# Four products of state and input weights computed in the first pair and kept in HBM, with new due steps for the first pair

## The chip, the cores and the metric

The kernel runs on one core of a Trainium2 chip. Its time is the device time of the whole program in microseconds (us), from several runs. Beside these there is one profiled execution, from which all lines of the profile come. Engines are called PE (TensorE, matrix products), PEld (its weight loads), DVE (VectorE), ACT (ScalarE), POOL (GpSimd) and SP (SyncE, whose queue issues nearly all DMAs).

## The reference

A cross attention between tokens and a small state, in both directions, whose outputs are laid together and go through a gated layer. `x` and `state` are float32; `w_in` (512 x 2048) and `w_out` (2048 x 512) are float64.

```python
B, H, S, Ns, D = 8, 8, 512, 32, 64           # x: (B,H,S,D), state: (B,H,Ns,D)
a  = softmax(scale * x @ state.T);  xread = a @ state      # 512 rows per batch
a2 = softmax(scale * state @ x.T);  sread = a2 @ x         # 32 rows per batch
y = concat([xread, sread], axis=2) -> (B*(S+Ns), H*D)      # 4352 x 512
h = y @ w_in;  g = h * cos(h);  out = g @ w_out            # 4352 x 2048, 4352 x 512
```

## The kernel before, in words

**The token rows.** `xread` is never formed. For each batch the state of each head is multiplied with the rows of `w_in` of that head ("products": 8 small matmuls of 64 rows and 32 columns, which run beside each other on PE, for 512 columns of `w_in`), so that `h` is the product of the attention weights `aT` with these products `sw`. A batch needs four such products, `nt` = 0 to 3, one for each 512 columns. `Attention.products(nt)` makes one in two banks of PSUM, either `at` or `side_banks`; `products_kept(nt)` copies it with ACT to `sw_all[:, nt % 2]`. So `sw_all` has two slots, used in turn, and product `nt` + 2 can be written there when the tiles of product `nt` have read it. "(b, nt)" below is product `nt` of batch `b`.

**Tiles.** A tile is 128 columns of `h` for the 512 tokens of a batch: 16 tiles to a batch, four to a product. A tile goes through `hidden` (PE), `gate` (ACT, rounding), `gate2` (DVE), `gate3` (ACT, sine) and `gate4` (DVE), which writes `g_all`. From batch 2 on, two tiles are taken together and done with seven half-size products in place of eight (`seven_part`); four sums of `sw`, made by POOL three steps ahead (`sw_sums`), serve them. `g` times `w_out` is done for two batches at once ("pair"), as seven products p1 to p7 of half size, each again of seven stages; their 49 weight blocks lie in HBM in `blocks_kept` and are fetched by SP into a ring of four.

**Two planners.** A step is one tile; 128 steps for the tokens, then 16 for the state rows.
- *The first pair* (batches 0 and 1, steps 0 to 31). It also loads and converts the float64 weights: each piece is loaded raw and converted by two operations of ACT, two of DVE and one of POOL. The w_out blocks' sums and their stores to `blocks_kept` are made here too, and the first five stages of p5 with the first tile pair of batch 2. The first two products with `w_out` are done plainly here, eight steps each: `first` (into `held` slot 0) and `second` (into slot 1, `second_kept`; its result is stored). All work is listed as tasks with a cost, what they read and write, and a due step. `first_pair` turns due steps to times (22 + PACE x step), passes them back along dependencies, and takes on each engine, among tasks that can start within NEAR, the one due first. Tasks that use the same buffer keep the order in which they are listed. `FIRST` = 32 and `now[0]` is 31 here.
- *The later pairs* (from step 32). The program is written step by step to a tape; `in_order` orders it again by a model of costs. `plan(b)` says at which step of a batch its products are made: (b, 1) at 0, (b, 2) at 3, (b, 3) at 8, (b + 1, 0) at 12. There the banks `at` are used.

`held` has three slots of 128 x 2 x 512 for partial results of the output (slot 0 is first the raw state).

Of the kernel before, what the change touches and what calls it, by code (L numbers as in the profile page):

```python
# [10 lines left out]
F32 = mybir.dt.float32  # L11
# [11 lines left out]
def kernel(  # L23
# [44 lines left out]
    nc = Lanes  # L68
# [42 lines left out]
    def matrix(n):  # L111
# [7 lines left out]
            for i in range(NB)]  # L119
    spare = ctx.enter_context(tc.tile_pool(name="spare", bufs=1,  # L120
                                           space=bass.MemoryType.DRAM))
    blocks_kept = spare.tile([7, 8, P, QT * P], F32)

    xT = consts.tile([P, NK, S], F32)
    ots_all = [consts.tile([P, S], F32, name=f"ot{i}") for i in range(2)]
    n_stored = [0]
    x_b = consts.tile([P, NC, H, D], F32)
# [157 lines left out]
    class Attention:  # L285
# [891 lines left out]
    def first_pair_tasks():  # L1177
# [49 lines left out]
        def attention(b, k):  # L1227
# [89 lines left out]
        def products(b, nt, k, c0=0, c1=WC):  # L1317
# [16 lines left out]
            for j in range(2):  # L1334
# [5 lines left out]
                        nc.vector.tensor_copy if taken else None, (j,)),  # L1340
                    side[j], sw[j], k)

        def tile_(t, k):
            n = t.b * NF + t.f
            h, z, c = n % 2, t.b % 2, t.f // 4 % 2
            g = names(quads_of[t.row][t.i // QT], t.i % QT)
            add("pe", 1.72, lambda: hidden(t),
                f"sw{c}{t.f % 4 // 2}0 sw{c}{t.f % 4 // 2}1 z{z}0 z{z}1",
                f"h{h} H", k)
            add("act", act(512) - .04, lambda: gate(t), f"h{h}", f"q{h}")  # L1350
            add("dve", dve(512) - .02, lambda: gate2(t), f"h{h} q{h}", f"q{h}")
            add("act", .63 if n else 1.91, lambda: gate3(t), f"q{h} T",
                f"q{h}")
            add("dve", dve(512) - .02, lambda: gate4(t), f"h{h} q{h}", g,
                k + 2)

        def inner(which, m, q, temps, to, k, raw=True):
            for i in range(4):
                t = to.split()
                r = (names(q), names(q) + " " + t[0], names(q),  # L1360
                     names(q) + " " + t[1])[i]
                add("pool", pool(512), lambda i=i: inner_weight(m, temps, i),
                    r, t[i], k)
            if raw:
                sends(which, m, q, k + 1)
            for i in range(4):
                add("sp", .4, lambda i=i: send_inner(which, temps, i),
                    to.split()[i], f"B{which}", k + 1)
# [135 lines left out]
                lambda i=i, due=due: conversion(i, due))  # L1504
        for step, what in (
                (1, lambda: attention_late(0, 0)),
                (3, lambda: products(0, 1, 2.5)),
                (3, lambda: add("pe", .4, lambda: states(1, side_banks[0]),
                                "held0", "sd00 sd01", 8.5)),
                (3, lambda: add("act", .53,  # L1510
                                lambda: states_kept(1, side_banks[0]),
                                "sd00 sd01", "stT1", 5.5)),
                (5, lambda: attention(1, 4)),
                (7, lambda: products(0, 2, 4.5)),
                (11, lambda: products(0, 3, 11.5)),
                (13, lambda: products(1, 0, 16)),
                (13, lambda: attention_late(1, 18)),
                (13, lambda: inner(0, a11, 5, temps[0], names(TEMPS), 14.5)),
                (15, lambda: sends(2, a22, 8, 17)),
                (15, lambda: sums_of(SQ, A21, A22, add_, 16, "pool")),  # L1520
                (16, lambda: products(1, 1, 18.5)),
                (16, lambda: inner(3, matrix(SQ), SQ, temps[1], E, 17)),
                (17, lambda: sums_of(A22, SQ, A11, sub_, 16, "pool")),
                (17, lambda: attention(2, 19)),
                (18, lambda: sums_of(A21, A11, A21, sub_, 20, "dve")),
                (20, lambda: products(1, 2, 23)),
                (20, lambda: inner(5, matrix(A21), A21, temps[0],
                                   names(TEMPS), 20)),
                (20, lambda: sends(1, a12, 6, 22)),
                (21, lambda: inner(4, matrix(A22), A22, temps[1], E, 22)),  # L1530
                (23, lambda: sums_of(SQ, A12, A22, sub_, 23, "dve")),
                (24, lambda: inner(6, matrix(SQ), SQ, temps[0], names(TEMPS),
                                   25)),
                (24, lambda: products(1, 3, 31)),
                (25, lambda: attention_late(2, 25)),
                (24, lambda: [add("sp", .4, lambda n=n: fetch_block(n), "B3",
                                  f"ring{n}", 27) for n in range(NB - 1)])):
            at_step[step].append(what)
        t32, t34 = all_tiles[PERIOD], all_tiles[PERIOD + 2]
        for step, what in (  # L1540
                (26, lambda: outer(0, 2, 0, 0, 26, "dve")),
                (27, lambda: outer(0, 2, 0, 1, 27, "dve")),
                (28, lambda: tokens_of_next(32)),
                (28, lambda: products(2, 0, 28)),
                (28, lambda: p5_tasks(30.5)),
                (29, lambda: weight_columns(t32, 30.5)),
                (29, lambda: add("dve", .7, lambda: halves(2, 0), "z00 z01",
                                 "E0", 30, True)),
                (29, lambda: add("dve", .7, lambda: halves(2, 1),
                                 "z00 z01 E0", "E1", 30, True)),  # L1550
                (30, lambda: seven_tasks(t32, 29.5)),
                (31, lambda: weight_columns(t34, 32)),
                (32, lambda: outer(2, 3, 2, 0, 32, "dve")),
                (32, lambda: p3_sums(32))):
# [55 lines left out]
    def first_pair():  # L1610
# [23 lines left out]
        while can:  # L1634
# [28 lines left out]
            if t.shares or t.engine == "pool":  # L1663
                lock = end
            if t.engine == "sp":
                size = {"x": .13, "Q": 1.05, "B": .26, "r": .26}.get(
                    t.writes[0][0], .3)
                lanes = max(lanes, at_ + 1.3) + size / .36
                end = lanes - 1.8
# [296 lines left out]
```

## Time and profile before

| what | value |
|---|---|
| runs | median 719.63 us of 3 (718.04 to 723.23) |
| profiled execution | 716.66 us, its span 714.9 us, granted clock 1.00 |
| products in the later pairs (PE at<-w_in,st_all) | 384 records of 64x512, 16 to a product |
| products in the first pair (PE h<-w_in,st_all) | 112 records of 64x512, 32 of 64x256 |
| ACT copies of products from at / from h | 48 / 16 |
| HBM read, written | 87.03 MB, 23.59 MB |
| first pair on PE | to about 151 us |

The busy time of an engine is the union of its instructions; a matmul record has 379 ns for 256 columns[...]. Each matmul in float32 appears as two records. Where a line ends in brackets, they hold the idle time of that engine just before it and the engine and tile whose end released it.

### The profile page before, as it was taken

The page shows a single profiled execution, that of the slowest core. Times are in us where ns is not written, and L with a number is a line of the kernel's source. Part 1 is how long each engine was busy: PE and PEld are TensorE (multiplying, and loading weights), DVE is VectorE, ACT ScalarE, POOL GpSimd, SP SyncE. Part 2 cuts the span into 40 slices and gives each one's busy share as a digit, 9 for nine tenths or more (in the row PEclk, how much of TensorE's full clock was granted, in tenths as well). Part 3 has the DMA queues.
Part 4 walks back from the last instruction along what each step waited for, and adds up shares of the span by engine and source line. Part 5 has one row for each costly group of instructions (what it writes and reads, how often), then busy time and mean ns, then how long its engine had stood idle before and what let it go on. Part 6 is the DMA issues. An engine that isn't in the chain of part 4 may idle for free.

```text
span 714.9 us, 10741 instructions
## 1 busy us (share of the span) xinstructions
PE 696.3 (97%) x3628; PEld 520.8 (73%) x3628; DVE 487.8 (68%) x698; ACT 348.2 (49%) x591; POOL 518.7 (73%) x524
## 2 busy tenths in 40 slices
PE   8898799999999999999999999999999999999997
PEld 3344344477878787787778788877888888888886
DVE  4999879977867578877776576868765465624430
ACT  5789876754544465443744473345444443211100
POOL 1565799576889988798889746789888748695500
PEclk9999999999999999999999999999999999999999
DMA  9966699765458744772369337843365344376841
GB/s 296 298 209 197 193 265 292 177 154 142 125 138 180 192 139 114 148 174 79 93 133 196 92 88 140 173 117 89 118 169 141 90 118 118 104 220 169 222 97 30
DMA packets 204022, 111.34 MB, mean 156 GB/s; under 512 B 149888, under 2 KB 166784, under 8 KB 203968
## 3 DMA queue, kind: packets, MB, share of 16 engines
q1 hardware_dynamic: 202880, 110.14, 59.2%
q8 instruction: 29, 0.48, 0.3%
q10 hardware_dynamic: 960, 0.39, 0.2%
q14 instruction: 25, 0.20, 0.1%
q0 software_dynamic: 128, 0.13, 0.1%
HBM read 87.03 MB, written 23.59 MB: 155 GB/s over the span
## 4 chain that ended last, share of the span: by engine, by line
PE 66%; DVE 2%; ACT 1%; POOL 1%; issue 1%; ACTq 0%; DVEq 0%
PE o L51 38%; PE h L51 21%; PE at L51 8%; POOL g_all L51 1%; ACT q_all L51 1%; DVE g_all L51 1%; DVE h L51 0%; DVE q_all L51 0%; DVE xT L51 0%; ACT L51 0%; DVE aT_all L51 0%; DVE held L51 0%; DVE m_all L51 0%; ACT sw_all L51 0%; ACT aT_all L51 0%
## 5 line engine op out<-in xcount | busy, mean ns | idle before, releaser
L51 POOL TENSOR_TENSOR g_all<-g_all 128x512 f32<-128x512 f32 x280 | 354.9, 1296 | 43.2 <-DVE g_all L51 17.5
L51 PE MATMUL o<-g_all 128*128 128x256 f32 (+1 forms) x1560 | 383.9, 391 | 0.0
L51 PEld LDWEIGHTS o<-g_all 128*128 128x128 f32 x1560 | 293.2, 190 | 63.9 <-issue 21.8
L51 ACT ACTIVATE q_all<-h 128x1024 int32<-128x1024 f32 (+1 forms) x88 | 73.2, 831 | 120.8 <-PE h L51 119.2
L51 DVE TENSOR_TENSOR q_all<-q_all,h 128x1024 f32<-128x1024 int32 (+1 forms) x88 | 85.5, 973 | 62.7 <-ACT q_all L51 62.4
L51 PE MATMUL h<-aT_all,sw_all 128*128 128x256 f32 (+1 forms) x320 | 118.1, 469 | 5.4 <-DVE g_all L51 5.4
L51 DVE TENSOR_TENSOR g_all<-h,q_all 128x1024 f32<-128x1024 f32 (+1 forms) x88 | 85.8, 977 | 38.3 <-ACT q_all L51 36.6
L51 ACT ACTIVATE q_all<-q_all,halfpi 128x1024 f32<-128x1024 f32 (+1 forms) x88 | 84.1, 957 | 35.9 <-DVE q_all L51 35.2
L51 PEld LDWEIGHTS h<-aT_all,sw_all 128*128 128x128 f32 x320 | 59.2, 190 | 40.7 <-issue 20.6
L51 DVE TENSOR_TENSOR g_all<-g_all 128x1024 f32<-128x1024 f32 (+1 forms) x78 | 74.3, 993 | 0.1
L51 DVE TENSOR_TENSOR h<-h,sums_all 128x256 f32<-128x256 f32 x96 | 41.1, 428 | 38.5 <-PE h L51 33.5
L51 PE MATMUL h<-aS_all,swS_all 128*128 128x256 f32 x192 | 59.7, 393 | 0.0
L51 PE MATMUL h<-aS_all,sw_all 128*128 128x256 f32 x192 | 57.5, 381 | 1.2 <-DVE h L51 1.0
L51 POOL TENSOR_TENSOR swS_all<-sw_all 128x128 f32<-128x128 f32 x48 | 21.9, 457 | 48.1 <-ACT sw_all L51 28.6
L51 PEld LDWEIGHTS h<-aS_all,swS_all 128*128 128x128 f32 x192 | 34.4, 189 | 21.3 <-issue 8.2
L51 PEld LDWEIGHTS h<-aS_all,sw_all 128*128 128x128 f32 x192 | 35.9, 190 | 7.9 <-DVE h L51 1.6
L51 POOL TENSOR_TENSOR w_in<-w_in,aS_all 128x1024 int32<-128x1024 int32 (+1 forms) x10 | 21.4, 2153 | 27.9 <-ACT m_all L51 14.2
L51 DVE SCALAR_TENSOR_TENSOR held<-o,held 128x512 f32<-128x512 f32 x38 | 26.1, 687 | 15.0 <-PE o L51 14.3
L51 ACT COPY sw_all<-at 128x512 f32<-128x512 f32 x48 | 25.8, 591 | 18.6 <-PE at L51 18.2
L51 ACT COPY o<-o 128x256 f32<-128x256 f32 x26 | 9.3, 359 | 46.7 <-PE o L51 46.6
L51 ACT COPY o<-sums_all 128x256 f32<-128x256 f32 x26 | 9.8, 376 | 44.9 <-PE o L51 44.9
L51 POOL TENSOR_TENSOR g_all<-g_all,aS_all 128x1024 int32<-128x1024 int32 x8 | 20.9, 2627 | 13.6 <-DVE g_all L51 7.2
(99 smaller groups left out, 748.6 us busy)
## 6 DMA issues: line engine op xcount, KB each, us to landing
g_all<-blocks_kept SPq DMA_DIRECT2D x206, 256.0 KB, 2.8
blocks_kept<-g_all SPq DMA_DIRECT2D x48, 256.0 KB, 4.1
g_all<-in_moe_w_out_dram SPq DMA_DIRECT2D x8, 1024.0 KB, 5.7
out_dram<-ot SPq DMA_DIRECT2D x128, 64.0 KB, 2.8
g_all<-in_moe_w_in_dram SPq DMA_DIRECT2D x6, 1024.0 KB, 7.6
x_b<-in_x_dram SPq DMA_DIRECT2D x24, 256.0 KB, 4.8
xT<-in_x_dram SPq DMA_DIRECT2D x80, 64.0 KB, 2.9
x_b<-in_x_dram SPq DMA_DIRECT2D x16, 128.0 KB, 4.0
```

Source lines behind the costliest of these rows:

```text
L51: made = self.last = f(*args, **kw)
```

## The change

- The products (3, 0), (3, 1), (2, 2) and (2, 3) are made in the first pair, in `side_banks`. ACT copies each to a slot of `held` (1 or 2, in turn), and SP sends it from there to a new array `products_early` in HBM (512 KB each).
- In the later pairs these four are not made: `products` returns, and `products_kept` is a DMA by SP from `products_early` into the slot of `sw_all`.
- The due steps of the first pair's tasks are other numbers, as are PACE, NEAR and the spacing passed back along dependencies, the order and due steps of the weight conversions, and the times at which the planner takes the raw weights to have arrived.

```diff
     blocks_kept = spare.tile([7, 8, P, QT * P], F32)
+    EARLY = ((3, 0), (3, 1), (2, 2), (2, 3))
+    EARLY_DUE = (13.61, 17.22, 27.33, 28.44)
+    products_early = spare.tile([len(EARLY), P, 2 * S], F32)
...
         def products(self, nt, bank=None, c0=0, c1=WC):
+            if now[0] >= FIRST and (self.b, nt) in EARLY:
+                return
...
         def products_kept(...):
+            if now[0] >= FIRST and (self.b, nt) in EARLY:
+                nc.sync.dma_start(
+                    out=sw_all[:, nt % 2].rearrange("p j s -> p (j s)"),
+                    in_=products_early[EARLY.index((self.b, nt))])
+                return
...
-    ARRIVED = (10.0, 11.3, 12.7, 14.0, 16.6, 19.3, 22.0)
+    ARRIVED = (10.7, 12.1, 13.5, 14.8, 18.2, 20.9, 23.9)
...
-            m2 = k + 6 if b == 0 else k + 4
+            m2 = k + 6 if b == 0 else k + 8.0
...
+        def products_ahead(n):
+            b, nt = EARLY[n]
+            slot, k = 1 + n % 2, EARLY_DUE[n]
+            w = ("w0 w1 w2 w3", "w4 w5", "w7 w8", "w10 w11")[nt]
+            side = ["sd00 sd01", "sd10 sd11"]
+            add("pe", 1.05, lambda: attn[b].products(nt, 0),
+                w + f" stT{b // 4}", " ".join(side), k)
+            for j in range(2):
+                add("act", act(WC), lambda j=j: nc.scalar.copy(
+                    held[:, slot, j], side_banks[j]), side[j],
+                    f"held{slot}{j}", k)
+            add("sp", .5, lambda: nc.sync.dma_start(
+                out=products_early[n],
+                in_=held[:, slot].rearrange("p j s -> p (j s)")),
+                f"held{slot}0 held{slot}1", f"p{n}", k + 2)
...
             add("dve", dve(512) - .02, lambda: gate4(t), f"h{h} q{h}", g,
-                k + 2)
+                k + 23.5)
...
-                (3, lambda: products(0, 1, 2.5)),
+                (3, lambda: products(0, 1, 8.5)),
...
-                (7, lambda: products(0, 2, 4.5)),
-                (11, lambda: products(0, 3, 11.5)),
-                (13, lambda: products(1, 0, 16)),
-                (13, lambda: attention_late(1, 18)),
+                (7, lambda: products(0, 2, 14.0)),
+                (11, lambda: products(0, 3, 14.0)),
+                (13, lambda: products(1, 0, 21.5)),
+                (13, lambda: attention_late(1, 35.0)),
...
-                (16, lambda: products(1, 1, 18.5)),
+                (16, lambda: products(1, 1, 32.0)),
...
-                (17, lambda: attention(2, 19)),
+                (17, lambda: attention(2, 17.5)),
...
-                (20, lambda: products(1, 2, 23)),
+                (20, lambda: products(1, 2, 24.5)),
...
-                (24, lambda: products(1, 3, 31)),
+                (24, lambda: products(1, 3, 28.5)),
...
-                (28, lambda: products(2, 0, 28)),
+                (28, lambda: products(2, 0, 34.0)),
...
+        for n, due in enumerate(EARLY_DUE):
+            at_step[max(0, int(due) - 1)].append(
+                lambda n=n: products_ahead(n))
...
-                first(step - 4, step - 1)
+                first(step - 4, step + 1)
             for i in range(NH):
                 if SECOND_AT[i] == step:
-                    second(i, step)
+                    second(i, step - 2)
...
-    CONV = (4, 5, 6, 7, 8, 9, 10, 11, 14, 15, 16, 17, 12, 13)
-    CONV_DUE = (3, 4.5, 3.5, 6, 6.7, 8.5, 9, 9.5, 12.0, 11, 11.3, 13.7, 12.5, 15.7)
-    PACE, NEAR, SEND = 3.4, 0.3, 2.5
+    CONV = (4, 6, 5, 7, 9, 8, 10, 11, 14, 15, 16, 17, 13, 12)
+    CONV_DUE = (1.8, 1.5, 1.0, 3.0, 5.3, 5.0, 12.4, 7.7, 14.1, 10.0, 12.0, 16.0, 17.1, 16.4)
+    PACE, NEAR, SEND = 3.2, 0.15, 2.5
...
-                t.due = min(t.due, u.due - t.cost - 0.05)
+                t.due = min(t.due, u.due - t.cost - 0.3)
```

The other due steps that change are those of the sums, stores and inner weights of `w_out`, of the second half of the states, of batch 1's and 2's attention, and of the tasks from step 26 on; the kinds of work are the same.

More of the change, by code (lines that the diff above doesn't have):

```diff
@@ L122 @@
     blocks_kept = spare.tile([7, 8, P, QT * P], F32)
+    EARLY = ((3, 0), (3, 1), (2, 2), (2, 3))
+    EARLY_DUE = (13.61, 17.22, 27.33, 28.44)
+    products_early = spare.tile([len(EARLY), P, 2 * S], F32)
     xT = consts.tile([P, NK, S], F32)
+    hbm_names.append(products_early.name)
     ots_all = [consts.tile([P, S], F32, name=f"ot{i}") for i in range(2)]
@@ L1506, in first_pair_tasks @@
                 (1, lambda: attention_late(0, 0)),
-                (3, lambda: products(0, 1, 2.5)),
+                (3, lambda: products(0, 1, 8.5)),
                 (3, lambda: add("pe", .4, lambda: states(1, side_banks[0]),
-                                "held0", "sd00 sd01", 8.5)),
+                                "held0", "sd00 sd01", 7.0)),
                 (3, lambda: add("act", .53,
                                 lambda: states_kept(1, side_banks[0]),
-                                "sd00 sd01", "stT1", 5.5)),
@@ L1513, in first_pair_tasks @@
-                (5, lambda: attention(1, 4)),
-                (7, lambda: products(0, 2, 4.5)),
-                (11, lambda: products(0, 3, 11.5)),
-                (13, lambda: products(1, 0, 16)),
-                (13, lambda: attention_late(1, 18)),
-                (13, lambda: inner(0, a11, 5, temps[0], names(TEMPS), 14.5)),
-                (15, lambda: sends(2, a22, 8, 17)),
-                (15, lambda: sums_of(SQ, A21, A22, add_, 16, "pool")),
-                (16, lambda: products(1, 1, 18.5)),
@@ L1522, in first_pair_tasks @@
-                (16, lambda: inner(3, matrix(SQ), SQ, temps[1], E, 17)),
-                (17, lambda: sums_of(A22, SQ, A11, sub_, 16, "pool")),
-                (17, lambda: attention(2, 19)),
-                (18, lambda: sums_of(A21, A11, A21, sub_, 20, "dve")),
-                (20, lambda: products(1, 2, 23)),
+                                "sd00 sd01", "stT1", 2.5)),
+                (5, lambda: attention(1, 4.5)),
+                (7, lambda: products(0, 2, 14.0)),
+                (11, lambda: products(0, 3, 14.0)),
@@ new lines, in first_pair_tasks @@
+                (13, lambda: products(1, 0, 21.5)),
+                (13, lambda: attention_late(1, 35.0)),
+                (13, lambda: inner(0, a11, 5, temps[0], names(TEMPS), 17.5)),
+                (15, lambda: sends(2, a22, 8, 17)),
+                (15, lambda: sums_of(SQ, A21, A22, add_, 31.5, "pool")),
+                (16, lambda: products(1, 1, 32.0)),
+                (16, lambda: inner(3, matrix(SQ), SQ, temps[1], E, 16.0)),
+                (17, lambda: sums_of(A22, SQ, A11, sub_, 18, "pool")),
@@ L1527, in first_pair_tasks @@
+                (17, lambda: attention(2, 17.5)),
+                (18, lambda: sums_of(A21, A11, A21, sub_, 22.5, "dve")),
+                (20, lambda: products(1, 2, 24.5)),
                 (20, lambda: inner(5, matrix(A21), A21, temps[0],
-                                   names(TEMPS), 20)),
+                                   names(TEMPS), 23.0)),
                 (20, lambda: sends(1, a12, 6, 22)),
-                (21, lambda: inner(4, matrix(A22), A22, temps[1], E, 22)),
-                (23, lambda: sums_of(SQ, A12, A22, sub_, 23, "dve")),
+                (21, lambda: inner(4, matrix(A22), A22, temps[1], E, 41.0)),
@@ L1532, in first_pair_tasks @@
+                (23, lambda: sums_of(SQ, A12, A22, sub_, 30.0, "dve")),
                 (24, lambda: inner(6, matrix(SQ), SQ, temps[0], names(TEMPS),
                                    25)),
-                (24, lambda: products(1, 3, 31)),
-                (25, lambda: attention_late(2, 25)),
+                (24, lambda: products(1, 3, 28.5)),
+                (25, lambda: attention_late(2, 25.0)),
                 (24, lambda: [add("sp", .4, lambda n=n: fetch_block(n), "B3",
@@ L1540, in first_pair_tasks @@
         for step, what in (
-                (26, lambda: outer(0, 2, 0, 0, 26, "dve")),
-                (27, lambda: outer(0, 2, 0, 1, 27, "dve")),
-                (28, lambda: tokens_of_next(32)),
-                (28, lambda: products(2, 0, 28)),
+                (26, lambda: outer(0, 2, 0, 0, 28.0, "dve")),
+                (27, lambda: outer(0, 2, 0, 1, 32.5, "dve")),
+                (28, lambda: tokens_of_next(32.0)),
+                (28, lambda: products(2, 0, 34.0)),
                 (28, lambda: p5_tasks(30.5)),
-                (29, lambda: weight_columns(t32, 30.5)),
+                (29, lambda: weight_columns(t32, 33.5)),
                 (29, lambda: add("dve", .7, lambda: halves(2, 0), "z00 z01",
@@ L1550, in first_pair_tasks @@
                                  "z00 z01 E0", "E1", 30, True)),
-                (30, lambda: seven_tasks(t32, 29.5)),
+                (30, lambda: seven_tasks(t32, 30)),
                 (31, lambda: weight_columns(t34, 32)),
@@ L1665, in first_pair @@
             if t.engine == "sp":
-                size = {"x": .13, "Q": 1.05, "B": .26, "r": .26}.get(
+                size = {"x": .13, "Q": 1.05, "B": .26, "r": .26, "p": .52}.get(
                     t.writes[0][0], .3)
```

## Prediction

> **What bounds the kernel now.** I read four views: the page, busy time in stretches of 10 us, the tensor engine's (PE's) timeline, and ACT's timeline where PE waits. First the page: busy rows, and slices of 17.9 us.
>
> ```profile
> PE 696.3 (97%) x3628; PEld 520.8 (73%) x3628; DVE 487.8 (68%) x698; ACT 348.2 (49%) x591; POOL 518.7 (73%) x524
> ...
> PE   8898799999999999999999999999999999999997
> ...
> PEclk9999999999999999999999999999999999999999
> ```
>
> PE is the bound, at full clock; slices under 9 lie only at the very end and before 130 us, in the first pair. Stretches there, with the columns PE, weight load, DVE, ACT, POOL, clock, DMA share, GB/s:
>
> ```profile
> 60.00:70.00 10.00, 8.09 (x25) 3.90 (x24) 8.99 (x14) 9.15 (x14) 5.00 (x2) 1.00 0.59 184
> 70.00:80.00 10.00, 7.99 (x46) 2.60 (x45) 9.36 (x14) 8.80 (x16) 6.31 (x3) 1.00 0.61 195
> 80.00:90.00 10.00, 7.77 (x60) 3.50 (x59) 7.79 (x11) 8.98 (x14) 7.90 (x5) 1.00 0.54 159
> ...
> 100.00:110.00 10.00, 10.00 (x47) 4.53 (x45) 8.05 (x10) 4.83 (x9) 9.99 (x6) 1.00 0.69 208
> 110.00:120.00 10.00, 10.00 (x37) 4.00 (x37) 10.00 (x15) 6.31 (x11) 9.84 (x8) 1.00 0.96 283
> ```
>
> From 60 to 92 us ACT and DVE are nearly full and PE has holes; from 92 us on PE is full. The holes in PE's timeline (start, length, operation; in brackets the idle time before it and who ended it):
>
> ```profile
> 67.47 1.98 PE L51 MATMUL h<-aT_all,sw_all 128*128 128x512 f32 x4 [1.91 <-DVE g_all L51]
> ...
> 74.90 1.98 PE L51 MATMUL h<-aT_all,sw_all 128*128 128x512 f32 x4 [1.00 <-DVE g_all L51]
> ...
> 78.91 3.70 PE L51 MATMUL h<-aT_all,sw_all 128*128 128x512 f32 x8 [1.01 <-DVE g_all L51]
> ...
> 87.73 1.09 PE L51 MATMUL at<-x_b,xT 128*64 128x128 f32 x16 [1.16 <-ACT xT L51]
> 89.89 1.98 PE L51 MATMUL h<-aT_all,sw_all 128*128 128x512 f32 x4 [1.07 <-DVE g_all L51]
> ```
>
> PE waits for the last gate operation of an earlier tile (DVE g_all), which frees a bank of h, and once for a copy by ACT. The five holes are 6.15 us. Earlier ones are 2.63, 0.85 and 0.21 us, later ones 0.34 and 0.41: 10.6 us between 20 and 146 us. Filler matmuls (o<-g_all at 20.03, 30.55 and 34.08 us) are 4.0 us more. **The rule of my sum**: PE's work stays as large as it was; four pieces of it move. So the end moves by idle time filled or made, and by nothing else.
>
> **What is removed.** One product of the later pairs, batch 2's third, in PE's timeline:
>
> ```profile
> 171.22 0.59 PE L51 MATMUL h<-aT_all,swS_all 128*128 128x256 f32 x2
> 171.74 1.09 PE L51 MATMUL at<-w_in,st_all 64*32 64x512 f32 x16
> 172.76 1.99 PE L51 MATMUL o<-g_all 128*128 128x256 f32 x8
> 174.59 0.59 PE L51 MATMUL h<-aS_all,sw_all 128*128 128x256 f32 x2
> ```
>
> From start to start it takes 1.02 us. The group before it takes 0.52 where such a pair otherwise takes 0.43, and the eight after it 1.83 where they otherwise take 1.73: 0.19 us more. [...] By the bare row the four products are 4 x 1.02 = 4.1 us, with the switches 4 x 1.21 = 4.84. I take 4.84. [...]
>
> The four stand at 171.74, 197.21, 217.57 and 235.30 us, in a PE that is full, so the 4.84 us leave the path whole. The second has a hole behind it:
>
> ```profile
> 198.44 1.08 ACT L51 COPY sw_all<-at 128x512 f32<-128x512 f32 x2 [2.00 <-PE at L51]
> 199.54 1.28 ACT L51 ACT_TABLE_LOAD   x1
> 200.83 1.15 ACT L51 ACTIVATE q_all<-q_all,halfpi 128x1024 f32<-128x1024 f32 x1
> ```
>
> ACT waited 2.00 us for this product, copied it, and only then loaded the table for the sine; through DVE that ended PE's wait of 0.88 us before 203.70. Without the copies ACT is up to 3 us earlier there and the hole goes: **-0.88**. What is late next is PE itself.
>
> **What is added late: four loads of 512 KB.** Each writes a slot of sw_all as soon as its last reader is done. I read these times from PE's timeline as 165.5, 184.4, 204.2 and 224.3 us, with the next readers 18 to 20 us later. POOL's four sums (0.46 us each) stand between load and reader. The rows for 256 KB:
>
> ```profile
> g_all<-blocks_kept SPq DMA_DIRECT2D x206, 256.0 KB, 2.8
> blocks_kept<-g_all SPq DMA_DIRECT2D x48, 256.0 KB, 4.1
> ```
>
> Twice the bytes land in 2.8 to 5.6 us, my estimate: at least 10 us are spare. Issuing takes SP 0.4 us each. A load that waits for its slot holds the ring fetches behind it on SP; these are issued three stages ahead, about 8 us at 2.7 us a stage (565 us for 206), and land in 2.8, so 5 us of waiting cost nothing. Bounds 0 to 2 us for all four, taken as 0.
>
> **What is added in the first pair.** Per product: 1.21 us of PE, two ACT copies (1.05 us by the pair sw_all<-h at 78.91), one send on SP of 0.4 us. They share the side banks with the others, in the order of listing: batch 3's first product goes between batch 0's fourth (72.8 us) and batch 1's first (76.8), its second between batch 1's second (83.6) and third (115.6), batch 2's pair after batch 1's fourth (126.3).
> - Batch 3's two fall where the holes are: PE 0 (2.42 of the 6.15 us are filled). ACT gets 2.1 us more in a stretch where it is busy 24.87 of 28 us (64 to 92). If all of it delays gates, it costs 2.1; if it fits into ACT's 3.1 us of idle time, 0. I take **+0.6**, nearer to 0: batch 1's first product, copied at 78.91 and first read at 93.43, now has due step 21.5 for 16, and its 1.05 us of copies can leave the stretch.
> - Batch 2's two fall where PE is idle 0.76 us in 54 (92 to 146): **+2.42**. Bounds 0, if later work is pulled into the holes, to 2.42.
> - The sends wait for ACT's copies; behind them on SP stand block sends and token loads, which have 5 us and more. Taken as 0; where it isn't, see the last rival.
>
> **Due steps set anew.** The operations stay, their order changes. Its worth is bounded by idle time: 6.15 - 2.42 + 0.75 = 4.5 us gained if every remaining hole after 60 us closes, 3.8 lost if two new ones like the longest (1.91) open. For a gain speak products copied long before use: batch 0's third ran at 50.52 and was first read at 61.09, with ACT at 9.2 of 10; its due goes from step 4.5 to 14. I take half of the gain: **-2.2**.
>
> **Sum**: -4.84 - 0.88 + 2.42 + 0.6 - 2.2 = -4.9 us. The profiled execution took 716.66 us (span 714.9 and 1.8 around it) and would take 711.8. The runs shown have a median of 719.63, 3 us above the profiled one; the same step from there gives **714.7 us**, 0.7% less.
>
> **Rivals.**
> - *The new order closes the holes.* All of 6.15 + 0.75 goes, half of the 4.0 us of filler, and the 0.88: -9.8, 709.8 us. For it: PE's idle time in 60 to 92 us is larger than what the two products need, and copies done 10 to 15 us early are there to be shifted. Against: ACT is at 89% there, DVE at 81%.
> - *The first pair gives it back.* ACT's 2.1 us delay the gates in full and the new order brings nothing: -4.84 - 0.88 + 2.42 + 2.1 = -1.2, 718.4 us.
> - *Slower: a send holds up the accumulator.* Batch 2's third product is kept in slot 1 of held, listed ahead of the end of the second product, which writes that slot next. ACT's copy of the accumulator (at 125.56 now) then waits until the send has landed; behind it on ACT stand all gates, and p5's first stage on PE (133.65) waits for the bank. If that product runs at 127.5, copies end at 129, and the send lands 4.1 (the row of half its size) to 8.2 us later, the copy ends at 134.6 to 138.7, so p5 starts up to 5.2 us late. [...] the DMA share was 0.97 from 120 to 130 us. With the 9.0 us between p5's first two stages (133.65 and 142.68) no longer covered by tiles 28 to 30, I add 4 us: 9.2 - 2.7 (the sum without the new order) = +6.5, 726 us. It decides when the accumulator's copy starts after about 135. Against it: the planner knows the dependency and can do the product earlier.
> - *That it doesn't do what it says* I exclude: the skip holds from step 32 on, the products in the first pair are made at 31, and all four are planned at steps 35 to 48.
>
> **How the numbers follow.** Forecast 0.49, with its own range 711 to 718; about a quarter of it (0.13) lies under 712.4, the point of 1%, which is about what a measurement of this kernel can tell from no change. Holes closed 0.31, all faster; given back 0.08, all same; slower 0.12, two thirds of it beyond 1%. So faster 0.31 + 0.13 = 0.44, slower 0.08, same the remaining 0.48. The range takes in most of the holes-closed case and the bounds above (ACT's 2.1, the loads' 2): 706.5 to 720.5.
>
> **What would show it.** PE at<-w_in,st_all falls from 384 to 320 and h<-w_in,st_all of 512 columns rises from 112 to 176; ACT sw_all<-at from 48 to 40. The hole before 203.70 is gone, and from the end of the first pair on the kernel takes 5.7 us less. Holes between 60 and 92 us sum to 2 us or less; the step to the later pairs (p5's first stage) comes no later than 134. I am wrong if that stage comes after 137, if new waits for POOL swS_all or sw_all appear on PE after 165, or if the stretch after the first pair is no shorter.

## The result, and the profile after

The changed kernel takes 716.58 us (median of 19 executions, 714.95 to 718.81), the kernel before 719.63 us (19 executions, 716.9 to 723.97). The ratio is 0.9953 with a 95% interval of 0.9936 to 0.997. The forecast was 714.7 us: right in direction, in its range and in the outcome "within 1%", and 1.9 us too low. The profiled execution takes 715.76 us, only 0.9 us less than the one of before (716.66), where the prediction had 711.8. So there are two questions: why an execution at full clock gains so much less than forecast, and where the other 2 us of the medians come from.

The products have moved as planned: 64 records fewer in the later pairs (384 before), 64 more in the first pair (112 before).

```profile
L51 PE MATMUL at<-w_in,st_all 64*32 64x512 f32 x320 | 22.1, 600 | 0.0
L51 PE MATMUL h<-w_in,st_all 64*32 64x512 f32 x176 | 12.0, 600 | 0.6 <-ACT sw_all L51 0.6
```

A record has 600 ns, and PE's timeline has the 16 records of a product within 1.09 us (161.73 us): so the eight matmuls of a product do run beside each other.

The page of the changed kernel, the rows of PE:

```profile
PE 698.5 (98%) x3632; PEld 522.6 (73%) x3632; DVE 487.5 (68%) x698; ACT 348.8 (49%) x591; POOL 515.5 (72%) x524
...
PE   8799899999999999999999999999999999999997
```

A slice is 17.9 us. The fourth and fifth, from 54 to 89 us, rose from 8 and 7 to 9 and 8; the second, from 18 to 36 us, fell from 8 to 7. In stretches of 10 us (PE, weight load, DVE, ACT, POOL, clock, DMA share, GB/s):

```profile
30.00:40.00 10.00, 7.14 (x48) 2.96 (x47) 6.75 (x13) 8.70 (x11) 4.65 (x3) 1.00 1.18 318
...
60.00:70.00 10.00, 10.00 (x25) 4.44 (x24) 8.13 (x11) 9.09 (x13) 5.08 (x2) 1.00 0.60 210
70.00:80.00 10.00, 9.30 (x69) 3.31 (x67) 9.11 (x15) 9.25 (x16) 5.07 (x3) 1.00 0.37 108
80.00:90.00 10.00, 8.85 (x71) 3.96 (x61) 8.47 (x10) 7.86 (x12) 8.34 (x4) 1.00 0.85 276
90.00:100.00 10.00, 9.06 (x42) 4.06 (x41) 6.53 (x9) 8.81 (x22) 8.01 (x5) 1.00 1.02 288
```

PE was busy 8.09, 7.99 and 7.77 us of 10 from 60 to 90 us; now it is 10, 9.30 and 8.85. The longest single wait ("hole") of the first pair was at 24 us before,

```profile
24.27 1.09 PE L51 MATMUL at<-x_b,xT 128*64 128x128 f32 x16 [2.63 <-ACT xT L51]
```

and is at 35 us now. Of the waits in PE's timeline of the first pair these are the largest up to 92 us:

```profile
35.39 1.98 PE L51 MATMUL h<-aT_all,sw_all 128*128 128x512 f32 x4 [2.86 <-DVE g_all L51]
...
77.44 1.98 PE L51 MATMUL h<-aT_all,sw_all 128*128 128x512 f32 x4 [0.70 <-DVE g_all L51]
...
81.10 1.98 PE L51 MATMUL h<-aT_all,sw_all 128*128 128x512 f32 x4 [0.65 <-DVE g_all L51]
...
85.62 1.98 PE L51 MATMUL h<-aT_all,sw_all 128*128 128x512 f32 x4 [0.49 <-DVE g_all L51]
```

From 60 to 92 us the waits sum to 1.85 us, for 6.15 before.

**The balance of the profiled execution.** Batch 2's second product is made in both kernels at the start of the later pairs; it starts at 158.73 us before and at 161.73 us now. So the first pair is 3.0 us longer, and what follows to the end of the span is 3.9 us shorter (714.9 - 158.7 = 556.2 against 714.0 - 161.7 = 552.3).
- First pair: 4.84 us of products came in. Waits fell by 3.6 us: by 4.3 from 60 to 92 us, by 0.35 from 20 to 60, while 92 to 150 has 0.9 more (1.67 for 0.76) and the start 0.16 more. Filler (matmuls of zeros, whose results nobody reads, which the planner puts where it expects PE to idle before the first product with `w_out`) grew from 8 to 12 records of 512 columns, each of which starts 0.43 us after the one before it: 1.7 us. 4.84 - 3.6 + 1.7 = 2.9, for the 3.0 that is seen.
- Later: PE's busy time fell by 4.4 us (551.1 to 546.7 by the view of stretches from that start on), where 4.84 was forecast, and waits rose by 0.5 us (0.88 to 1.40 from 150 to 320 us). 4.4 - 0.5 = 3.9.

**The clock.** Every execution of the runs below, and of the changed kernel, is listed with its mean granted clock. The kernel before spreads over 7 us, and its time goes with the clock (medians; three executions of before and one of the changed kernel with other means are left out):

| mean clock | before (75 executions beside the first four experiments) | changed (19 executions) |
|---|---|---|
| 1.000 | 717.0 us, 17 of them | 715.7 us, 5 |
| 0.998 | 718.6, 12 | 716.1, 5 |
| 0.997 | 719.8, 3 | 717.6, 4 |
| 0.995 | 719.6, 18 | 718.0, 4 |
| 0.993 | 722.8, 22 | none |

So at full clock the change is worth 1.3 us. The mean over all executions is 0.9961 before and 0.9977 now. In the table 0.007 of clock go with 5.8 us before, so 0.0016 are worth about 1.3 us more, my estimate; the remaining 0.4 of the 3.05 us is no more than the spread. (The 19 executions of before that ran beside the changed kernel have no clock on record; the 75 have nearly their median, 719.06.) Experiment 5 is about what lowers the clock.

### The profile page after: what moved, and what is told of

The parts are those of the page before. It is cut to its first block, busy times and chain, and to the rows that moved or that the text cites. A ratio compares the mean times of both kernels' runs of the same rounds, so it can differ in the third digit from the quotient of the medians.

```text
span 714.0 us, 10772 instructions
## 1 busy us (share of the span) xinstructions
PE 698.5 (98%) x3632; PEld 522.6 (73%) x3632; DVE 487.5 (68%) x698; ACT 348.8 (49%) x591; POOL 515.5 (72%) x524
## 4 chain that ended last, share of the span: by engine, by line
PE 88%; ACT 4%; DVE 3%; DMA 3%; issue 1%; SPq 0%; POOL 0%; DVEq 0%; ACTq 0%
PE o L51 47%; PE h L51 31%; PE at L51 10%; DMA g_all<-in_moe_w_out_dram 2%; ACT q_all L51 1%; DVE g_all L51 1%; ACT L51 1%; DVE i_all L51 1%; DMA x_b<-in_x_dram 1%; ACT sr L51 1%; ACT aS_all L51 0%; ACT sw_all L51 0%; SPq L51 0%; DVE xT L51 0%; DVE q_all L51 0%
## 5 line engine op out<-in xcount | busy, mean ns | idle before, releaser
L51 DVE TENSOR_TENSOR g_all<-g_all 128x1024 f32<-128x1024 f32 (+1 forms) x78 | 71.7, 960 | 0.1
L51 POOL TENSOR_TENSOR swS_all<-swS_all,sw_all 128x128 f32<-128x128 f32 x48 | 23.9, 498 | 12.4 <-PE o L51 2.9
```

Of the source, the lines that this page charges most:

```text
L51: made = self.last = f(*args, **kw)
```

## The experiments

**1. The products without the new due steps, and the new due steps without the products.** The first kernel has EARLY, `products_ahead` and the loads, and all other numbers as before (EARLY_DUE scaled to PACE 3.4). The second has

```diff
-    EARLY = ((3, 0), (3, 1), (2, 2), (2, 3))
+    EARLY = ()
```

> The kernel before with the four products made in the first pair and loaded later, and every other due step as before. Theory (moved work): from the end of the first pair to the end 3.9 us are saved, as in the changed kernel; the first pair gets longer by the two products of batch 2 (2.4) and part of ACT's copies (0 to 2.1). So a profiled execution of 715 to 717 us and a ratio to before of 0.995 to 1.000. Rival (the new due steps bring the gain): the first pair gets longer by at least what is saved later; 717 us or more, ratio 1.000 to 1.004.

> The changed kernel with no product moved: the new due steps alone. Theory (moved work): no part of the 3.9 us saved later; the first pair changes by less than 1 us; profiled execution 716 to 717.5 us, ratio 0.999 to 1.001. Rival (the new due steps bring the gain): the first pair ends 1.8 us or more earlier, profiled execution 715 us or less, ratio 0.996 or less.

Measured: the products alone take 718.1 us, ratio 0.9972 (0.9954 to 0.9991): somewhat faster, as the theory of moved work has it. Their mean clock is 0.9961, that of before, so this 1.0 us is no gain of the clock. (The profiled execution, 718.11 us, lies above the 715 to 717 expected; it has two stretches at half clock, one before 20 us and one in the ten behind it, whose mean is 0.83.) The due steps alone take 722.61 us, ratio 1.0039 (1.0023 to 1.0055): slower, which neither theory expected. PE's timeline of the due steps alone:

```profile
126.66 1.98 PE L51 MATMUL h<-aT_all,sw_all 128*128 128x512 f32 x4 [1.17 <-DVE g_all L51]
131.09 3.54 PE L51 MATMUL h<-aT_all,sw_all 128*128 128x512 f32 x4 [2.44 <-DVE g_all L51]
134.55 1.97 PE L51 MATMUL at<-x_b,xT 128*64 128x128 f32 x32
```

With the due steps alone the holes from 60 to 92 us shrink to 2.5 us, with the products alone they are still 5.6: it is the due steps that close most of them. The four more filler records come with the due steps too; the products alone have as many as before. But from 92 to 150 us 6.0 us of waits open. Neither half gives what both give: as far as this pair shows, the due steps fit the set of tasks that they were set for.

**2. Half of the products.** The changed kernel with two of the four:

```diff
-    EARLY = ((3, 0), (3, 1), (2, 2), (2, 3))
+    EARLY = ((3, 0), (3, 1))        # the other: ((2, 2), (2, 3))
```

> The changed kernel with batch 3's two products moved alone. Theory (idle time filled): these two lie in the holes of the first pair and cost nothing there, so all of their 2 x 1.21 us is kept: this kernel is as fast as the changed one or faster by up to 1 us, ratio to before 0.994 to 0.997. Rival (ACT's copies are the price): it is slower than the kernel with batch 2's two products.

> The changed kernel with batch 2's two products moved alone. Theory (idle time filled): these two lie where the tensor engine is full, so what is saved later (2.4 us) is paid in the first pair: as the new due steps alone, within 1 us of before, ratio 0.998 to 1.001. Rival (ACT's copies are the price): faster than the kernel with batch 3's two, since ACT has room after 100 us.

Measured: batch 3's two alone 721.17 us, ratio 1.0017 (0.9999 to 1.0036); batch 2's two alone 717.02 us, 0.9959 (0.9945 to 0.9974), nearly the whole change. My theory had it the other way round. That is the order which the rival (ACT's copies) foretold, but copies and sends are too small for it: all four products' together are worth 0.7 us in experiment 3, and these two kernels lie 4.15 us apart. What the traces show is PE's waits from 92 to 150 us: 6.0 us with no product moved, 4.2 with batch 3's, 1.8 with batch 2's, 1.7 with all four. With batch 3's two the longest is:

```profile
131.33 1.99 PE L51 MATMUL h<-aT_all,sw_all 128*128 128x512 f32 x4 [3.49 <-DVE g_all L51]
```

From 150 to 320 us batch 3's two have 2.75 us of waits (1.40 before 160.31 and 1.35 before 209.11 us, both for DVE h), batch 2's two 0.87: in the later pairs, too, the planner finds the worse order for batch 3's two. Batch 2's products, listed at the end of the first pair, change the order in which the first planner does that end. That this comes from due times passed back along their dependencies is only my reading; it wasn't tried.

**3. What the four cost in the first pair.** The plan of the changed kernel is kept, but parts of the early tasks are not issued, so that nothing else changes place. In the first kernel matmuls, copies and sends are left out, in the second copies and sends; in both the loads read rows of x.

```diff
-            add("pe", 1.05, lambda: attn[b].products(nt, 0),
+            add("pe", 1.05, lambda: None,      # second kernel: as before
...
-                add("act", act(WC), lambda j=j: nc.scalar.copy(
-                    held[:, slot, j], side_banks[j]), side[j],
+                add("act", act(WC), lambda: None, side[j],
```

> The changed kernel with its order kept and the four products' matmuls, copies and sends of the first pair left out; the later loads read rows of x instead, so the output for those columns is not the reference's. It shows what the four cost in the first pair. Theory (idle time filled): about half of their 4.84 us is paid there, so this kernel's first pair ends 2 to 3 us earlier than the changed one's, profiled execution 712.5 to 713.5 us. Rival (the tensor engine's price is paid whole and ACT's on top): 4.8 us or more earlier, 711 us or less.

> As the kernel without early work, but with the four products' matmuls made in the first pair; ACT's copies and the sends are left out, and the loads read rows of x. Theory (the tensor engine pays): within 0.5 us of the changed kernel. Rival (ACT's copies pay): within 0.5 us of the kernel without early work, 1.5 us or more below the changed one.

Measured: 715.07 us (4 executions) without any early work in the first pair, 715.88 us (6 executions) with the matmuls alone, for 716.58 with everything. The whole of it costs 1.5 us by the medians, less than the 2 to 3 us expected, and 0.5 us between executions at full clock (715.24, a single one, and 715.7); with 4 and 6 executions it isn't settled more finely. In the profiled execution with matmuls alone batch 2's second product starts at 160.94 us, for 161.73 in the changed kernel: by this pair of traces copies and sends cost 0.8 us. So, by these few executions, in an order that is fixed most of the 4.84 us lies in waits that are there anyway. The 0.7 us between the medians with matmuls alone and with everything lies between the theory (0.5 at most) and the rival (1.5 or more).

**4. The return without and with the order of before.** First the changed kernel with the four products made in the later pairs too:

```diff
-            if now[0] >= FIRST and (self.b, nt) in EARLY:
-                return                      # and the load in products_kept
```

> The changed kernel's first pair, with the four products made and sent there, and all of them made again in the later pairs: the cost of the added work without its return. Theory: 3.0 us longer than before at the end of the first pair, and nothing saved: profiled execution 719.5 to 720 us, ratio 1.003 to 1.005. Rival (the first pair's added work is hidden): within 1 us of before.

Measured: 720.5 us, ratio 1.0011 (0.9997 to 1.0025). From the first half-size product of batch 2 to the end it takes 568.43 us, for 564.85 in the changed kernel and 568.75 before: the loads in place of the products save 3.6 us there, and the added work without return makes the kernel no faster than before. The ratio lies below the 1.003 to 1.005 expected; at full clock it is 719.2 us (3 executions) against 716.9 (6 of before beside it), which is 1.003.

Then the changed kernel with the later pairs ordered as if the four products were still there (planned, but not issued):

```diff
-                    tape.append((self, op, f, args, kw, burst[0]))
+                    tape.append((self, op, None if ghost[0] else f, args, kw,
+                                 burst[0]))
...
-                return                      # products and copies of the four
+            ghost[0] = now[0] >= FIRST and (self.b, nt) in EARLY
```

> The changed kernel, but the later pairs are ordered as if the four products and copies were still there (they are planned and not issued; the loads are). Theory (the new order of the later pairs keeps a hole): the waits of the tensor engine near 201, 205 and 266 us (0.25, 0.62 and 0.53) go and the one of before near 203 (0.88) does not come back; from the end of the first pair to the end 4.8 to 5.7 us less than before, instead of 3.9. Rival (the hole at 203 was not ACT's copies): a wait of 0.5 us or more stays near 200 us and the saving is within 0.5 us of 3.9.

Measured: 717.46 us, ratio 0.9973 (0.9957 to 0.9989), and the same stretch takes 566.70 us: 2 us saved for 3.9. PE's timeline has, in place of the hole near 203 us,

```profile
206.83 0.70 PE L55 MATMUL h<-aS_all,swS_all 128*128 128x256 f32 x2 [1.49 <-POOL swS_all L55]
...
240.45 0.67 PE L55 MATMUL h<-aS_all,sw_all 128*128 128x256 f32 x2 [0.80 <-DVE h L55]
```

The theory falls: the old order doesn't take the hole away, another engine ends it. The rival's wait stays, but its saving of about 3.9 us does not. Around 200 us, where ACT does batch 3's exponentials, there are waits of 0.87 us or more in sum in these orders: before, changed, made twice and this one. They aren't bound to be there: with the due steps alone PE waits 0.07 us in all from 150 to 320 us.

**5. What lowers the clock.** A second trace of the kernel before:

> The kernel before, for a second trace. Its executions spread from 717 to 724 us, and the longer ones have a lower mean clock. Theory (half clock after holes): in this trace, if its mean clock is under 1, PEclk is below 1 in one or more stretches of about 3.4 us near the start, behind the wait near 24 us, or among the holes from 60 to 92 us, and PE's work there takes twice as long; with a mean clock of 1.000 the span is again within 0.5 us of 714.9. Rival (the spread is in the DMAs): the late part of the trace differs instead.

It took 722.94 us, at a mean clock of 0.993, and its span is 721.2 us, 6.3 more than the first. Its stretches (columns as above, the clock is the third number from the end), and PE's timeline at the same places:

```profile
25.00:30.00 5.00, 5.00 (x19) 2.29 (x16) 2.60 (x4) 1.24 (x4) 3.25 (x2) 0.66 0.98 371
...
70.00:75.00 5.00, 5.00 (x9) 2.07 (x8) 4.93 (x8) 4.32 (x6) 0.81 (x1) 0.66 0.19 71
...
95.00:100.00 5.00, 5.00 (x10) 2.15 (x9) 1.52 (x3) 2.99 (x7) 4.84 (x5) 0.77 1.23 295
```

```profile
24.53 1.09 PE L51 MATMUL at<-x_b,xT 128*64 128x128 f32 x16 [2.76 <-ACT xT L51]
25.55 5.40 PE L51 MATMUL h<-aT_all,sw_all 128*128 128x512 f32 x8
...
69.43 3.24 PE L51 MATMUL h<-aT_all,sw_all 128*128 128x512 f32 x4 [1.92 <-DVE g_all L51]
...
91.39 1.09 PE L51 MATMUL at<-x_b,xT 128*64 128x128 f32 x16 [1.16 <-ACT xT L51]
93.56 3.47 PE L51 MATMUL h<-aT_all,sw_all 128*128 128x512 f32 x4 [1.07 <-DVE g_all L51]
```

Right behind a wait the same four records take 3.24 and 3.47 us for 1.98, the eight 5.40 for 3.70. Three stretches at half clock (the first trace's clock record has the shares 1.0 and 0.5 alone). In each of the first two, 0.34 x 5 = 1.7 us of full clock are missing by the stretches above, and as much in the third, which begins before 95 us (0.89 from 90 to 95 us): at half clock 3.4 us each. With 6.3 us more of span that is about 2.1 each. Of these 6.3 us, 5.1 are half of the 3 x 3.4 us, and PE's waits are 1.2 us longer as well. From the first half-size product of batch 2 on, the two traces agree to 0.04 us (568.79 and 568.75). So in these two traces the whole difference comes from the first pair, and a hole costs more than its own length when the clock falls behind it. The trace of the due steps alone above is another one: 3.54 us for four records behind a wait of 2.44, at a mean clock of 0.83 from 125 to 135 us.

Not every stretch costs as much. Made twice has the changed kernel's first pair, with a stretch at half clock at 35 us (0.68 from 35 to 40 us) that the changed kernel's own trace lacks (1.00); batch 2's second product starts at 162.75 us there, for 161.73: 1.0 us. In two traces the clock is lower before 20 us already: 0.91 and 0.92 in the first two stretches of 10 us with the products alone, 0.90 and 0.93 with the due steps alone, again 1.7 us in sum; PE is busy only 6.6 and 6.8 of the first 10 us there. So the mean clock alone doesn't give the time.

The length of a wait doesn't tell by itself whether the clock falls. It fell behind waits of 2.76 us (at 24.53 us here, and at 25.33 us with the products alone), 2.69 (without early work), 2.44 (due steps alone) and 1.92 us. But in the first trace of the kernel before, waits of 2.63 and 1.91 us at the same places left it at 1.00, and it stayed up behind the changed kernel's wait of 2.86 us and behind 2.67 and 3.49 us with batch 3's two alone: the four records behind these three take 1.98, 1.98 and 1.99 us. What decides was not shown.

Then fillers in front of one wait in each kernel, with everything else in its place:

```diff
-                add("pe", 1.05, lambda j=j: a.reads(j), ...        # before
+                add("pe", 1.05, lambda j=j: (
+                    warm(3, acc[0]) if b == 0 and j == 0 else None,
+                    a.reads(j)), ...
...
-            add("pe", 1.72, lambda: hidden(t),                     # changed
+            add("pe", 1.72, lambda: (
+                warm(3, acc[0]) if n == 2 else None, hidden(t)),
```

> The kernel before with three filler matmuls (2.6 us) in front of the first read of batch 0, where the tensor engine idles 2.63 us near 24 us; nothing else changes. Theory (half clock after holes, and this one among them): the mean clock of its executions rises from 0.996 to 0.997 or more, its median falls by 0.7 to 1.7 us, ratio 0.997 to 0.999, with full-clock executions still at 717 us. Rival (the holes from 60 to 92 us do it): clock and median as before.

> The changed kernel with three filler matmuls (2.6 us) in front of tile 2, where the tensor engine idles 2.86 us near 35 us; nothing else changes. Theory (half clock after holes): no execution has half clock near 36 us any more, the mean clock rises from 0.9977 to 0.999, the median falls by 0.5 to 1.2 us to 715.4 to 716.1, ratio to before 0.993 to 0.995: faster than both kernels. Rival (half clock comes from the start of the program alone): as the changed kernel, 716.6 us.

Measured for the kernel before: 719.88 us, ratio 0.9998 (0.9982 to 1.0014): no gain. Its mean clock is 0.9971 (0.9960 of before's 28 executions beside it), so a little of the clock came back, but only 3 of 22 executions have 1.000. The time did not follow: with a mean clock of 0.998 it takes 719.8 us (11 executions), before 718.5 (7). That fits stretches of unlike cost, of which the filler took a cheap one; this was not tested. Its profiled execution has a mean clock of 0.998, too; the filler doesn't touch the holes from 60 to 92 us.

For the changed kernel: 715.78 us, ratio 0.9948 (0.9927 to 0.997), mean clock 0.9994, 7 executions from 714.86 to 716.84. The mean clock rose as expected. The 0.8 us to the changed kernel's 19 executions, made at another time, is within their spread and not settled by seven. The changed kernel has no other wait over 0.8 us after 20 us, and the clock doesn't fall where it did in the kernel without early work (1.00 from 35 to 40 us, for 0.66 there), whose trace has the wait at the same place:

```profile
35.35 3.23 PE L51 MATMUL h<-aT_all,sw_all 128*128 128x512 f32 x4 [2.69 <-DVE g_all L51]
```

With the fillers, PE's timeline there:

```profile
32.57 3.70 PE L51 MATMUL o<-g_all 128*128 128x512 f32 x8
36.10 1.88 PE L51 MATMUL h<-aT_all,sw_all 128*128 128x512 f32 x4
```

**6. The hole at 200 us.** In the changed kernel's trace ACT's sine there waits 2.54 us for DVE (q_all), which has a sum waiting for PE ahead of it. The kernel with fillers, and these two exchanged on DVE:

```diff
+        u, w = dves[gates[4] - 1], dves[gates[4]]
+        u.start, w.start = w.start, u.start
```

> The changed kernel with the three fillers in front of tile 2, and with one pair of operations exchanged on DVE: near 200 us the second gate operation (q_all<-q_all,h) goes ahead of the sum (h<-h,sums_all) that waits for the tensor engine. Theory (the hole near 205 us comes from DVE's order, not from ACT's copies of the products): the sine starts at about 199.5 instead of 202.06 us, the wait of 0.62 us for DVE g_all goes, and the stretch from the second pair's first tile to the end is 0.6 us shorter than the changed kernel's 564.85; median 715.0 to 715.8. Rival (ACT or the tensor engine's bank sets it): the sine starts at 202 and the wait stays.

Measured: 715.11 us (9 executions, 714.62 to 716.18), ratio 0.9944 (0.9922 to 0.9966), mean clock 0.9996. The sine starts 3.5 us earlier, at 198.57 us (1.0 of it because all of this trace is earlier), and yet the wait is there as before:

```profile
203.90 0.70 PE L51 MATMUL h<-aT_all,sw_all 128*128 128x256 f32 x2 [0.62 <-DVE g_all L51]
```

DVE shows why (start, length, operation):

```profile
199.44 0.43 DVE L51 TENSOR_TENSOR h<-h,sums_all 128x256 f32<-128x256 f32 x1 [1.35 <-PE h L51]
199.78 0.36 DVE L51 RECIPROCAL i_all<-i_all 128x34 f32<-128x34 f32 x1
201.16 0.43 DVE L51 TENSOR_TENSOR h<-h,sums_all 128x256 f32<-128x256 f32 x1 [1.02 <-PE h L51]
201.50 1.23 DVE L51 STREAM_TRANSPOSE xT<-i_all 128x1024 f32<-128x1024 f32 x1
202.66 1.18 DVE L51 TENSOR_TENSOR g_all<-h,q_all 128x1024 f32<-128x1024 f32 x1
```

The sine ends at 199.7, but the last gate operation stands in DVE's queue behind a second sum that waits for PE, and behind a transpose. So by its timeline DVE's order sets this wait, as the theory has it, but the pair that I exchanged was not the one that decides; putting that gate operation ahead of the sum and the transpose was not tried. The stretch from the first half-size product to the end is 564.79 us, unchanged; what little this kernel gains on the one with fillers alone lies within the executions' spread. The two are the fastest kernels here that compute the reference.

## Why the prediction was right or wrong, point by point

The number came out partly by luck. For an execution like the profiled one, at full clock, the prediction had 711.8 us, and it took 715.76: 0.9 us gained for 4.9. The 4.0 us between them are 0.4 in the products' size, 1.4 in the hole at 203 us and 2.2 in the first pair. That the medians differ by 3.05 us, nearer to the forecast, comes from a clock that the prediction has no term for.

- **The bound, and that PE's work only moves.** Right. Products in, waits out and filler in close to 0.1 us in the first pair. What the sum left out is that "idle time filled or made" includes filler, which the planner adds by itself.
- **-4.84 for the four products.** Right in kind, 0.4 too large. PE's busy time behind batch 2's second product fell by 4.4 us. By their bare rows the four are 4.07: from that product to the start of one at 312.65 us (311.77 now), counted from start to start, the groups of 64 rows take 6.12 us in place of 10.19. So the groups beside the products (0.52 us for 0.43 and 1.83 for 1.73 in the prediction, its "switches") brought some 0.35 us, where I had 0.76 from one product. In the first pair the balance closes with the full 4.84.
- **-0.88 for the hole at 203 us.** This step failed: +0.5 in its place. The copies went, but PE waits three times where it had waited once:

```profile
203.70 0.70 PE L51 MATMUL h<-aS_all,sw_all 128*128 128x256 f32 x2 [0.88 <-DVE h L51]
```

```profile
201.06 0.67 PE L51 MATMUL h<-aS_all,sw_all 128*128 128x256 f32 x2 [0.25 <-DVE h L51]
...
204.94 0.70 PE L51 MATMUL h<-aT_all,sw_all 128*128 128x256 f32 x2 [0.62 <-DVE g_all L51]
...
266.29 0.70 PE L51 MATMUL h<-aS_all,sw_all 128*128 128x256 f32 x2 [0.53 <-DVE h L51]
```

  The first is before, the others are now. By the timelines of experiment 6 it lies in DVE's order around batch 3's exponentials; I should have asked what stands ahead of the gate on DVE, not only on ACT. No order tried took it away, so this cause is argued, not shown.
- **0 for the loads.** Right: issued at 168.78, 186.48, 204.39 and 225.74 us, landed 3.4 to 5.3 us later, and no wait of PE after 150 us is put down to them.
- **The first pair: +2.42, +0.6 and -2.2, in sum +0.8.** Measured +3.0. Against 4.84 us of products the forecast had idle time fall by 4.0 us. Waits did fall by 3.6, but filler, taken as nothing, rose by 1.7, so that 1.9 us came off. The failing term is the -2.2 of the new due steps: they closed the holes from 60 to 92 us (6.15 to 1.85), but up to 43 us waits and filler together grew by 1.4 us, with 2.86 us in one place, and from 92 to 150 us waits grew by 0.9. Alone, the due steps cost 0.4% of the time. With these due steps batch 2's two products bring nearly the whole gain and batch 3's none, where I had it the other way round.
- **The signpost for the last rival.** I said that I'd be wrong if p5's first stage came after 137 us. It came at 142.24, and ACT's copy of the accumulator at 139.18 instead of 125.56. PE and ACT now:

```profile
142.24 1.89 PE L51 MATMUL o<-g_all 128*128 128x256 f32 x8
...
139.18 1.08 ACT L51 ACTIVATE held<-o 128x512 f32<-128x512 f32 x2
```

  The send ahead of it is in the order that I feared. Where batch 2's products are moved the copy starts between 136.6 and 142.7 us (batch 2's two, all four, the products alone); with batch 3's two or none, between 118.4 and 125.6. The send itself was quick: issued at 132.07, it landed 2.86 us later, below the prediction's 4.1 to 8.2, and ACT did other work until 139.18. The delay cost little, since PE had other work: its waits from 92 to 150 us sum to 1.67 us. The delay is real; the bound on what it costs was wrong.
- **What I did not see: the clock.** The forecast has no term for it. Of the gain of 3.05 us only 1.3 are left at full clock; most of the rest goes with a higher mean clock. Why the changed kernel keeps it more often, experiment 5 shows in part: its trace has one long hole in place of several, and with fillers in front of that one the mean clock was 0.9994 for 0.9977.

## What to carry to other kernels

If the bounding engine's work is only moved, count idle time, and count filler with it: here the sum of products, waits and filler closed to 0.1 us in the first pair and said at once which term was mis-sized. Compare a forecast made from one profile with the profile after it as well as with the medians: here the medians alone would have hidden a miss of 4 us. Due times set by search belong to one set of tasks; take them over with the set or not at all, and try each half before crediting either. Look at the spread of the executions and at their mean clock, not at one profile: here less than half of the gain is left at full clock, and most of the rest goes with a clock that falls behind waits in some executions and not in others. With three fillers in front of one wait of 2.9 us the mean clock was 0.9994 for 0.9977; in the kernel before, with other holes left, fillers gained no time.

## What the runs showed of the hardware

- PE's granted clock fell to one half for a stretch of 3.4 us behind a wait, in some executions and not in others: in the kernel before 17 of 75 had a mean clock of 1.000, 22 had 0.993. In traces such a stretch (0.66 as the mean of 5 us: 1.7 us of full clock missing) stood behind single waits of 2.76 (twice), 2.69, 2.44 and 1.92 us, and once behind a pair of 1.16 and 1.07 us that are 1.1 us of work apart.
- The length of a wait alone doesn't decide: behind waits of 3.49, 2.86, 2.67, 2.63 and 1.91 us the clock stayed up in other traces. What decides was not shown.
- A stretch cost about 2.1 us in the second trace of the kernel before, and 1.0 us at 35 us in the changed kernel's first pair (made twice).
- With filler matmuls in front of its one long wait the changed kernel's mean clock was 0.9994 (7 executions) for 0.9977 (19). They delayed the work behind them a little: tile 2 started at 36.10 us with them and at 35.39 without.
